# Routing loop: low halves on two engines, and one spread product per search step

## The chip, the cores and the metric

The kernel runs on one core of a Trainium2 chip. The metric is the device time of one execution in microseconds (us); the kernel before takes 1208.9 us in the median of three runs (1208.22 to 1209.22). The core has TensorE (PE in the profile; its weight loads are PEld), VectorE (DVE), ScalarE (ACT), GpSimd (POOL), and SyncE (SP), whose queue issues the plain DMA transfers. Each engine works through its own instructions in the order in which they were written; where one needs the result of another engine, it waits, and all behind it on that engine waits with it.

## The reference

Attention with a top-32 mask comes first (4 batches, 8 heads, 576 rows, 64 columns). Its output, 2304 tokens of 512 numbers, goes to eight experts: all token-expert scores are sorted from high to low, and a token goes to an expert if the token is still free and the expert has fewer than 288. Each expert computes max(x w1, 0) w2. At the end stands a rational function between two products with w_in and w_out.

```python
logits = x @ w_gate
order = np.argsort(-logits.flatten())
for idx in order:
    tok, e = int(idx) // E, int(idx) % E
    if assigned[tok] >= 0 or counts[e] >= cap:
        continue
    assigned[tok] = e
    counts[e] += 1
for e in range(E):
    h = np.maximum(x[assigned == e] @ w1[e], 0.0)
    out[assigned == e] = h @ w2[e]
# then: h = out @ w_in; g = P(h) / Q(|h|); result = g @ w_out
```

## The kernel before, in words

The products of the experts are exact to some 22 bits: each fp32 factor is scaled by a power of two and split into two fp16 halves, high and low, and three fp16 products are summed. For expert 0 the split of w1 and w2 (128 partitions x 4096 columns each) is made while the routing runs. `add_first` (line 1413) plans it: ScalarE writes the high half in chunks of 1024 columns (`conv_hi`, line 1357); for each block of 256 columns TensorE forms diag x raw - high in PSUM (`product`, line 1422: an fp32 product with a diagonal matrix of the scale, and an fp16 product with minus the identity), and ScalarE copies the result as the low half (`copy`, line 1428). These are 16 blocks for w1 and 16 for w2. The products use two PSUM banks in turn. When a weight's copies are done, `stage` (line 1398) fetches four more pieces of w_out into the room of the raw weight; these are the eight staged pieces.

The routing (`route`, line 1621) assigns tokens without sorting, in seven phases. In each phase `search` (line 1546) finds the score at which an expert becomes full, in four steps. A step compares all 2304 scores with 32 thresholds on VectorE (`cmp`, in two halves of nine columns), counts the hits per expert with 18 small matmuls, which follow one that subtracts what is needed (lines 1493 to 1509), lets VectorE mark which thresholds are over (`over`, line 1572, a tile of 32 partitions with nine columns), and spreads the weighted sum of these marks to all partitions with a matmul (`spread`, line 1551); VectorE makes the next 32 thresholds from it (`thr`, line 1584). In step i the spread sums the marks of steps 0 to i, with weights 1/32, 1/1024 and so on, so that it is a chain of i + 1 matmuls. The early ones of the chain are issued ahead of the marks of the last step. Between two phases VectorE runs a dozen short instructions (lines 1589 to 1678), GpSimd forms the selection, and 18 matmuls (line 1666) count it.

All other work near the routing is planned by a small list scheduler in Python, `Flow` (line 30). A task has an engine (A is ScalarE, V is VectorE, P is TensorE), an estimated cost, tasks it needs, and a rank; of the tasks that could start, the one with the earliest start and then the lowest rank is issued. In the search, `fill` (line 107) issues V tasks that fit into a budget (0.6 between cmp and over, 0.37 between over and thr, in the planner's units) and any A task that can start by then; `tail` (line 119) issues one P task after each spread. The plan of a step does not depend on whether a P task is in it. The preparation of w_in and w_out is planned the same way (`add_block`, line 420): pieces of 512 columns go through ScalarE (lines 374 to 386: the heads of a piece, with three ring buffers for some of them), VectorE (lines 396, 409, 413, for most pieces in two halves of 256 columns), ScalarE again (the norm, line 307), and in the end a split into high (line 437) and low halves (line 441, VectorE, longer than the budgets of the search). After the routing, the tokens of expert 0 are gathered, expert 0's products run, and the remaining blocks are finished beside them (`early`, line 148); then the pairs of hidden columns of the last two products follow for all experts (from line 2263).

Of the kernel before, what the change touches and what calls it, by code (L numbers as in the profile page):

```python
# [8 lines left out]
F32 = mybir.dt.float32  # L9
BF16 = mybir.dt.bfloat16  # L10
# [5 lines left out]
OP = mybir.AluOpType  # L16
# [13 lines left out]
class Flow:  # L30
# [69 lines left out]
    def use(self, cost):  # L100
        self.free["V"] += cost
        return self.free["V"]
# [69 lines left out]
def take(task, users, n, leave):  # L172

    task.takes.append((users, n))
    if not hasattr(task, "leaves"):
        task.leaves = {}
    task.leaves[id(users)] = leave
# [7 lines left out]
def kernel(  # L185
# [15 lines left out]
    nc = tc.nc  # L201
    B, H, S, D = q.shape
    N, DM = out.shape
    E = w_gate.shape[1]
    F1 = w1.shape[2]
    F2 = w_in.shape[1]
    P = 128
# [27 lines left out]
    consts = ctx.enter_context(tc.tile_pool(name="consts", bufs=1))  # L235
# [24 lines left out]
    GR = 32  # L260
    iota_r = consts.tile([P, GR], F32, name="iota_r")
    nc.gpsimd.iota(iota_r, pattern=[[1, GR]], base=0, channel_multiplier=0, allow_small_or_imprecise_dtypes=True)
    ITS, ITS_SLOW = 4, 7
    grids = consts.tile([P, ITS, GR], F32, name="grids")
    weights = consts.tile([GR, ITS], BF16, name="weights")
    fine_slow = consts.tile([P, ITS_SLOW], F32, name="fine_slow")
    for i in range(ITS):
        nc.vector.tensor_scalar(grids[:, i, :], iota_r, 1.0, float(GR) ** -(i + 1), op0=OP.add, op1=OP.mult)
        nc.vector.memset(weights[:, i : i + 1], float(GR) ** -(i + 1))
    for i in range(ITS_SLOW):  # L270
        nc.vector.memset(fine_slow[:, i : i + 1], 1.0 / (GR - 2) ** (i + 1))

# [38 lines left out]
    w_raw = {}  # L311
# [10 lines left out]
    w_sum, w_scale, w_split = {}, {}, {}  # L322
# [9 lines left out]
    flow = Flow()  # L332
# [3 lines left out]
    def fetch(slot, n=None):  # L336

        if n is None and todo and todo[0] <= slot[1]:
            n = todo.pop(0)
        if n is not None:  # L340
            nc.sync.dma_start(slot[0].bitcast(U16)[:, 0:2047], pieces[n][:, 1:2048])
            raw_t[n] = slot
            arrived[n].end = flow.transfer(1.5)
        elif slot[2] is not None:
            slot[2]()
# [130 lines left out]
    with ExitStack() as actx:  # L476
# [852 lines left out]
        def add_steps(steps, deps, rank, late=False):  # L1329

            done = []
            for engine, cost, fn, *takes in steps:
                t = flow.add(engine, cost, fn, deps, rank, late)
                if done and done[-1][1]:
                    take(done[-1][0], pa_users, 2, [t])
                done.append((t, takes))
                deps = [t]
            return deps[0]

        def scale_steps(which, e):  # L1340
            st = {}

            def total():
                st["t"] = ps_a.tile([P, 512], F32, name="pa")
                nc.tensor.matmul(st["t"][:, 0:4], ones, w_sum.pop((which, e)), start=True, stop=True)

            def reduce():
                w_scale[which, e] = [lpool.tile([P, 1], F32, name=f"w{n}{which}", bufs=5) for n in "si"]
                n2 = lpool.tile([P, 1], F32, name="wnorm", bufs=2)
                nc.vector.tensor_reduce(n2, st["t"][:, 0:4], axis=AX.X, op=OP.add)  # L1350
                st["steps"] = power_steps(*w_scale[which, e], n2, 380 + 2 * (11, 13)[which - 1])

            return [("P", 0.3, total, 1), ("V", 0.1, reduce)] + [
                ("V", 0.07, lambda i=i: st["steps"][i]()) for i in range(4)
            ]

        def conv_hi(which, e, c):
            if c == 0:
                w_split[which, e] = [lpool.tile([P, KC * F1], F16, name=f"w{which}s{i}") for i in range(2)]
            o = slice(c * 1024, (c + 1) * 1024)  # L1360
            nc.scalar.activation(w_split[which, e][0][:, o], w_raw[which, e][:, o], AF.Copy, scale=w_scale[which, e][0])
# [36 lines left out]
        def stage(which):  # L1398
# [11 lines left out]
            for i in range(4):  # L1410
                fetch((t[:, 1024 * i : 1024 * (i + 1)], -1, after), NP - 8 + 4 * (which - 1) + i)

        def add_first(which):

            scaled = add_steps(scale_steps(which, 0), [], -90.0)
            diag = npool.tile([P, P], F32, name=f"diag{which}", bufs=1)
            copies = [flow.add("A", 0.1, lambda: nc.scalar.activation(
                diag, ident, AF.Copy, scale=w_scale[which, 0][0]
            ), [scaled], -88.0)]
            bank = {}  # L1420

            def product(o):
                (h, l), src = (t[:, o : o + 256] for t in w_split[which, 0]), w_raw[which, 0][:, o : o + 256]
                pl = bank[o] = ps_l.tile([P, 512], F32, name="pl")[:, 0:256]
                nc.tensor.matmul(pl, diag, src, start=True, stop=False)  # L1425
                nc.tensor.matmul(pl, minus, h, start=False, stop=True)

            def copy(o):
                nc.scalar.activation(w_split[which, 0][1][:, o : o + 256], bank.pop(o), AF.Copy)

            for c in range(4):
                t = flow.add("A", 0.95, lambda c=c: conv_hi(which, 0, c), [scaled], -88.0)
                for o in range(c * 1024, (c + 1) * 1024, 256):
                    p = flow.add("P", 0.6, lambda o=o: product(o), [t, copies[0]], -88.0)
                    copies.append(flow.add("A", 0.27, lambda o=o: copy(o), [p], -90.0))
                    take(p, pl_users, 2, [copies[-1]])
            return flow.add("A", 0.0, lambda: stage(which), copies, -90.0)
# [20 lines left out]
        def routing(x, xs, lg, span, fast):  # L1458

            with ExitStack() as rctx:  # L1460
                rp = rctx.enter_context(tc.tile_pool(name="rp", bufs=1, side="right"))
                rw = rctx.enter_context(tc.tile_pool(name="rw", bufs=2, side="right"))
                psr = rctx.enter_context(tc.tile_pool(name="psr", bufs=2, space=PSUM))
# [43 lines left out]
                def compare(pc, need):  # L1507

                    nc.tensor.matmul(pc, ones_row[:, 0:GR], need[0:1, :], start=False, stop=True)

                CS = "9 9".split()
                CT, o = [], NT
# [33 lines left out]
                def search(edge, grid, vt, oh, need, fill, tail, use, until):  # L1546

                    rng, base = grid[0:2]
                    thr, overs = base[:, 0, :], []

                    def spread(pb, i, last):
                        nc.tensor.matmul(
                            pb, weights[:, i : i + 1].to_broadcast([GR, P]), overs[i], start=(i == 0), stop=last
                        )

                    for it in range(ITS):
                        if it == ITS - 1:
                            flow.free["G"] = max(flow.free["G"], flow.free["V"] + 4.5)
                        pc = counted(thr, vt, oh, need if it else None)
                        if it == 0:  # L1560
                            need, rest = need()
                            compare(pc, need)
                            rest()
                            use(0.4)
                        counts = use(C1) + 0.6
                        pb = psr.tile([P, 512], F32, name="pt")[:, 0 : E + 1]
                        for i in range(it):
                            spread(pb, i, False)
                        fill(J1 if it else J3)
                        until(counts)  # L1570
                        over = rw.tile([GR, E + 1], BF16, name="over8", bufs=ITS)
                        nc.vector.tensor_scalar(
                            over[:, 1:], pc, 0.0, None, op0=OP.is_ge, op1=OP.max, accum_out=over[:, 0:1]
                        )
                        overs.append(over)
                        spread(pb, it, True)
                        sums = use(0.07) + 0.36
                        tail(T1)
                        fill(J2)
                        until(sums)  # L1580
                        use(0.3)
                        if it < ITS - 1:
                            thr = rw.tile([P, GR], F32, name="thr")
                            nc.vector.scalar_tensor_tensor(
                                thr, rng.to_broadcast([P, GR]), pb[:, 0:1], base[:, it + 1, :], op0=OP.mult, op1=OP.add
                            )
                        else:
                            full = rw.tile([P, E], F32, name="full")
                            nc.vector.tensor_scalar(full, pb[:, 1:], pb[:, 0:1], None, op0=OP.is_equal)
                            nc.vector.tensor_scalar(edge, rng, pb[:, 0:1], span[:, 0:1], op0=OP.mult, op1=OP.add)  # L1590
                    return full
# [885 lines left out]
    with tc.If(nc.values_load(unusual[0:1, 0:1], min_val=0, max_val=P) != 0, preferred_fallthrough_block=False):  # L2477
# [7 lines left out]
        flow = Flow()  # L2485
# [40 lines left out]
```

## Time and profile before

| | before |
|---|---|
| median of three runs | 1208.9 us |
| the profiled execution, its own time | 1211.95 us |
| its span, first to last instruction | 1210.1 us |
| mean granted TensorE clock | 0.928 |

A window query sums, for each engine, the time in which it was busy in a stretch of the span; in a timeline row stand the start, the duration, the engine, the line, the operation, output<-input, and in brackets the idle time before with what ended it. "x2" stands for two like instructions in a row, whose duration then reaches from the first's start to the last's end. The granted clock is given in parts of full speed: 0.50 is the lower level, 1.2 GHz, and 1.00 the upper, 2.4 GHz.

### The profile page before, as it was taken

How to read it: one execution, taken by the hardware profiler on the slowest of the kernel's cores; microseconds unless marked ns; L12 is line 12 of the kernel's file. 1: busy time of each engine (PE TensorE's matmuls, PEld its weight loads, DVE VectorE, ACT ScalarE, POOL GpSimd, SP SyncE). 2: the span in 40 equal slices, each digit the busy share in tenths (PEclk: the TensorE clock that was granted, in tenths of full speed). 3: DMA queues.
4: the chain of work that ended last, by engine and by line, in shares of the span. 5: the costliest groups of instructions: out<-in, count | busy, mean ns of one | idle time of the engine just before them, and what ended most of it. 6: DMA issues, size and time to landing. Idle time of an engine off the chain costs nothing.

```text
span 1210.1 us, 26891 instructions
## 1 busy us (share of the span) xinstructions
PE 1118.0 (92%) x9758; PEld 902.8 (75%) x9758; DVE 1045.9 (86%) x4036; ACT 1019.4 (84%) x1816; POOL 385.6 (32%) x488
## 2 busy tenths in 40 slices
PE   5899999999999887995669999999999999999995
PEld 3688888888888765664547778888888888888774
DVE  6999999989889956878899888998989899897885
ACT  4899999989999796579999888888889887876684
POOL 4788888877778600003000010110000110001010
PEclk8899999999999995555889999999999999999998
DMA  5205212022000307413141302222211222000000
GB/s 126 53 10 157 46 25 51 23 48 51 3 2 2 140 1 281 159 54 100 62 159 71 140 27 86 88 90 78 97 66 32 90 91 84 8 2 21 1 21 23
DMA packets 81248, 80.64 MB, mean 67 GB/s; under 512 B 59985, under 2 KB 60113, under 8 KB 81105
## 3 DMA queue, kind: packets, MB, share of 16 engines
q1 hardware_dynamic: 78032, 69.34, 18.0%
q0 software_dynamic: 3072, 9.48, 2.7%
q8 instruction: 79, 1.29, 0.4%
q14 instruction: 65, 0.52, 0.1%
HBM read 69.25 MB, written 9.55 MB: 65 GB/s over the span
## 4 chain that ended last, share of the span: by engine, by line
PE 60%; DVE 18%; ACT 13%; issue 3%; POOL 3%; DMA 1%; SPq 0%; POOLq 0%; ACTq 0%; DVEq 0%
PE po L887 5%; PE po L2024 4%; PE po L2025 4%; PE po L2023 4%; PE ph L2023 4%; PE pa L2023 4%; PE ph L2025 4%; PE ph L2024 4%; PE pa L2024 4%; PE pa L2025 4%; DVE cd L753 4%; PE s L696 3%; PE pt L855 3%; DVE w L790 2%; PE pl L1425 2%
## 5 line engine op out<-in xcount | busy, mean ns | idle before, releaser
L789 POOL TENSOR_TENSOR win<-sv,sg 128x576 f32<-128x576 f32 x142 | 179.1, 1282 | 64.9 <-ACT sg L784 49.3
L753 DVE MAX8 cd<-sv 128x8 f32<-128x82 f32 (+1 forms) x1008 | 178.2, 230 | 11.5 <-ACT sv L706 11.4
L2023 PE MATMUL ph<-x,win 128*128 128x288 f16 x512 | 148.6, 290 | 7.2 <-DVE uv L2292 6.1
L887 PE MATMUL po<-vm,pT 128*128 128x65 f32 (+1 forms) x1280 | 150.7, 266 | 2.3 <-issue 1.1
L2024 PE MATMUL ph<-x,win 128*128 128x288 f16 x512 | 148.6, 290 | 0.0
L2025 PE MATMUL ph<-x,win 128*128 128x288 f16 x512 | 148.5, 290 | 0.0
L2024 PE MATMUL po<-g,wout 128*128 128x288 f16 x512 | 146.4, 286 | 2.3 <-DVE g L2014 2.3
L2023 PE MATMUL po<-g,wout 128*128 128x288 f16 x512 | 146.4, 286 | 1.4 <-ACT g L2013 1.3
L2025 PE MATMUL po<-g,wout 128*128 128x288 f16 x512 | 146.4, 286 | 0.0
L887 PEld LDWEIGHTS po<-vm,pT 128*128 128x128 f32 (+1 forms) x1280 | 138.6, 181 | 5.5 <-issue 1.9
L855 PE MATMUL pt<-ident,sv 128*128 128x128 f32 x648 | 125.7, 283 | 0.3 <-ACT pT L869 0.3
L859 PE MATMUL pt<-dg,mk 128*128 128x128 bf16 x720 | 120.0, 221 | 0.7 <-POOL mk L846 0.7
L2000 POOL DMA_INDIRECT xe<-xrows,rows_i x24 | 28.5, 1189 | 285.2 <-PE pa L2035 265.0
L784 ACT ACTIVATE sg<-sv,cut_all 128x576 bf16<-128x576 f32 x142 | 109.0, 778 | 5.7 <-DVE cut_all L759 5.7
L2283 ACT ACTIVATE z<-ph,inv 128x288 f32<-128x288 f32 x128 | 63.7, 497 | 57.8 <-PE ph L2025 54.9
L2413 POOL DMA_INDIRECT out_dram<-ob,tok x21 | 23.2, 1104 | 277.3 <-ACT ob L2409 223.0
L845 ACT ACTIVATE sg<-sv,pn 128x576 bf16<-128x576 f32 x136 | 97.9, 771 | 14.9 <-POOL pn L823 14.9
L696 PE MATMUL s<-region 64*128 64x288 f32 (+1 forms) x640 | 95.0, 450 | 14.9 <-ACT region L667 10.3
L790 DVE MAX8 w<-win 128x8 f32<-128x576 f32 x142 | 105.4, 743 | 0.0
L855 PEld LDWEIGHTS pt<-ident,sv 128*128 128x128 f32 x648 | 92.5, 143 | 15.8 <-issue 3.5
L846 POOL TENSOR_SCALAR mk<-sg 128x576 bf16<-128x576 bf16 x136 | 88.9, 671 | 1.8
L869 ACT ACTIVATE pT<-pt 128x1152 f32<-128x1152 f32 x72 | 81.4, 1131 | 3.1 <-PE pt L859 2.9
(364 smaller groups left out, 3309.2 us busy)
## 6 DMA issues: line engine op xcount, KB each, us to landing
region<-in_moe_w_dram SPq DMA_DIRECT2D x16, 2048.0 KB, 8.3
xrows<-x SPq DMA_DIRECT2D x1, 4644.0 KB, 21.8
region<-in_q_dram SPq DMA_DIRECT2D x32, 128.0 KB, 3.0
region<-in_k_dram SPq DMA_DIRECT2D x32, 128.0 KB, 3.0
vm<-in_v_dram SPq DMA_DIRECT2D x32, 128.0 KB, 3.1
wout<-in_moe_w_in_dram SPq DMA_DIRECT2D x8, 511.8 KB, 7.9
region<-in_moe_w_out_dram SPq DMA_DIRECT2D x8, 511.8 KB, 3.5
win<-in_moe_w_in_dram SPq DMA_DIRECT2D x6, 511.8 KB, 7.5
```

Source lines behind the costliest of these rows:

```text
L696: nc.tensor.matmul(sc[p0 : p0 + n, 2 * hh + g, 0:w], qT[rows, j, p0 : p0 + n], kT[rows, bb, c : c + w], start=True, stop=True,)
L753: nc.vector.max(cd[:, g, :], sv[:, o : o + n])
L784: nc.scalar.activation(sg, sv_t[u, hh], AF.Sign, bias=cut_all[:, 2 * u + hh, 7:8], scale=-OVER, accum_out=t["sum"][:, c : c + 1],)
L789: nc.gpsimd.tensor_tensor(win, sv_t[u, hh], sg, op=OP.mult)
L790: later.append(lambda c=c, win=win: nc.vector.max(t["w8"][:, c, :], win))
L845: nc.scalar.activation(sg, sv, AF.Sign, bias=t["pn"][:, c : c + 1])
L855: nc.tensor.transpose(dst, pr[:, c * P : (c + 1) * P], ident)
L859: nc.tensor.matmul(dst, mk_buf[u % 2][:, o : o + P], bat[b]["dg"][:, 2 * i + hh, :], start=False, stop=True, skip_group_check=True,)
L887: nc.tensor.matmul(po[p0 : p0 + n, i, hh, :], sb[:, hh * (R + 1) + c, p0 : p0 + n], vm[:, bb, hh, c, :], start=(c == 0), stop=False,)
L2023: nc.tensor.matmul(acc, ah, bh, start=first, stop=False)
L2024: nc.tensor.matmul(acc, ah, bl, start=False, stop=False)
L2025: nc.tensor.matmul(acc, al, bh, start=False, stop=last)
```

## The change

In `add_first`, of the blocks of 256 columns every second one (odd block numbers) no longer goes through TensorE and ScalarE: VectorE makes the low half from raw weight, scale and high half in one instruction. In `search`, the marks of the four steps stand in one tile of 128 partitions, 32 per step, and the weights in one column of 128 partitions, so that one matmul over 32, 64, 96 or 128 partitions takes the place of the chain of spreads.

```diff
-    weights = consts.tile([GR, ITS], BF16, name="weights")
+    weights = consts.tile([P, 1], BF16, name="weights")
...
-        nc.vector.memset(weights[:, i : i + 1], float(GR) ** -(i + 1))
+        nc.vector.memset(weights[GR * i : GR * (i + 1), :], float(GR) ** -(i + 1))
...
+        def rest_of(which, o):
+            h, l = w_split[which, 0]
+            nc.vector.scalar_tensor_tensor(
+                l[:, o], w_raw[which, 0][:, o], w_scale[which, 0][0], h[:, o], op0=OP.mult, op1=OP.subtract
+            )
+
...
                 for o in range(c * 1024, (c + 1) * 1024, 256):
+                    if o // 256 % 2:
+                        copies.append(flow.add("V", 0.37, lambda o=o: rest_of(which, slice(o, o + 256)), [t], -88.0))
+                        continue
                     p = flow.add("P", 0.6, lambda o=o: product(o), [t, copies[0]], -88.0)
...
-                    thr, overs = base[:, 0, :], []
-
-                    def spread(pb, i, last):
-                        nc.tensor.matmul(
-                            pb, weights[:, i : i + 1].to_broadcast([GR, P]), overs[i], start=(i == 0), stop=last
-                        )
-
+                    thr = base[:, 0, :]
+                    overs = rw.tile([GR * ITS, E + 1], BF16, name="over8")
...
-                        pb = psr.tile([P, 512], F32, name="pt")[:, 0 : E + 1]
-                        for i in range(it):
-                            spread(pb, i, False)
...
-                        over = rw.tile([GR, E + 1], BF16, name="over8", bufs=ITS)
+                        over = overs[GR * it : GR * (it + 1), :]
...
-                        overs.append(over)
-                        spread(pb, it, True)
+                        pb = psr.tile([P, 512], F32, name="pt")[:, 0 : E + 1]
+                        nc.tensor.matmul(
+                            pb, weights[0 : GR * (it + 1), :].to_broadcast([GR * (it + 1), P]),
+                            overs[0 : GR * (it + 1), :], start=True, stop=True,
+                        )
```

## Rows read from the trace of the kernel before

**Rows 1.** The page's first part: busy time, share of the span, instructions.
```profile
PE 1118.0 (92%) x9758; PEld 902.8 (75%) x9758; DVE 1045.9 (86%) x4036; ACT 1019.4 (84%) x1816; POOL 385.6 (32%) x488
```
**Rows 2.** Windows: routing, and what follows; stretch, length, busy by engine, clock, DMA.
```profile
core 0: us, PE busy (x) PEld busy (x) DVE busy (x) ACT busy (x) POOL busy (x), PEclk, DMA share, GB/s
...
462.30:555.20 92.90, 80.72 (x911) 55.53 (x912) 70.75 (x321) 67.63 (x113) 6.43 (x15) 0.50 0.46 165
555.20:645.00 89.80, 61.00 (x402) 43.82 (x402) 83.16 (x213) 85.63 (x158) 13.50 (x9) 0.82 0.31 103
```
**Rows 3.** Timeline, VectorE: a search step of the first phase.
```profile
466.38 0.26 DVE L1584 SCALAR_TENSOR_TENSOR thr<-rng,pt,base 128x32 f32<-128x32 f32 x1 [0.19 <-PE pt L1552]
466.67 0.83 DVE L1493 TENSOR_TENSOR cmp<-vt,thr 128x288 bf16<-128x288 f32 x2
...
467.99 0.16 DVE L1572 TENSOR_SCALAR_CACHE_REDUCE over<-pl 32x8 bf16<-32x8 f32 x1
...
468.41 0.26 DVE L1584 SCALAR_TENSOR_TENSOR thr<-rng,pt,base 128x32 f32<-128x32 f32 x1 [0.20 <-PE pt L1552]
```
**Rows 4.** Timeline, TensorE and VectorE: a search step of the second phase.
```profile
476.98 1.22 PE L1425 MATMUL pl<-region,diag 128*128 128x256 f32 x2
477.10 0.25 DVE L1584 SCALAR_TENSOR_TENSOR thr<-rng,pt,base 128x32 f32<-128x32 f32 x1
...
478.00 0.42 PE L1426 MATMUL pl<-w1s,minus 128*128 128x256 f16 x1
...
478.55 0.64 PE L1501 MATMUL pl<-oh,cmp 128*32 128x8 bf16 x18
479.12 0.49 PE L1552 MATMUL pt<-over,weights 32*128 32x9 bf16 x3
479.23 0.16 DVE L1572 TENSOR_SCALAR_CACHE_REDUCE over<-pl 32x8 bf16<-32x8 f32 x1 [0.68 <-PE pl L1501]
...
479.66 0.25 DVE L1584 SCALAR_TENSOR_TENSOR thr<-rng,pt,base 128x32 f32<-128x32 f32 x1
```
**Rows 5.** Waits (total, times, longest) and ScalarE's group of w2 copies, routing.
```profile
DVE over L1572 <- PE pl L1501: 11.4, 18, 0.7
ACT w1s L1429 <- PE pl L1426: 10.7, 8, 2.2
DVE nq L428 <- ACT junk L307: 2.0, 2, 1.7
...
L1429 ACT ACTIVATE w2s<-pl 128x256 f16<-128x256 f32 x16 | 6.2, 388 | 7.4 <-PE pl L1426 7.4
```
**Rows 6.** Groups of VectorE, 470 to 546 us: busy us, mean ns.
```profile
L396 DVE SCALAR_TENSOR_TENSOR ring<-wout,ring 128x256 uint16<-128x256 uint16 x16 | 7.0, 437 | 0.0
L409 DVE SCALAR_TENSOR_TENSOR wout<-wout,ring 128x256 uint32<-128x256 uint32 x16 | 6.6, 413 | 0.0
...
L409 DVE SCALAR_TENSOR_TENSOR win<-win 128x256 uint32<-128x256 uint32 x6 | 2.5, 414 | 0.0
```
**Rows 7.** Timeline: the end of the last phase.
```profile
545.21 0.67 PE L1666 MATMUL pt<-asel,onesb 128*128 128x8 bf16 x18
...
545.92 0.16 DVE L1678 TENSOR_TENSOR need<-cb,pt 128x8 f32<-128x8 f32 x1 [0.86 <-PE pt L1666]
```
**Rows 8.** VectorE after the loop: a timeline row, and two groups by line.
```profile
559.17 0.75 DVE L409 SCALAR_TENSOR_TENSOR nraw<-nraw,ring 128x256 uint32<-128x256 uint32 x2
...
L441 DVE SCALAR_TENSOR_TENSOR win<-wout,s_in,win 128x512 f16<-128x512 f32 x8 | 5.7, 733 | 0.0
...
L1366 DVE SCALAR_TENSOR_TENSOR w1s<-region,ws,w1s 128x1024 f16<-128x1024 f32 x8 | 10.1, 1276 | 0.0
```
**Rows 9.** ScalarE's group of staged pieces, and VectorE's waits, after the loop.
```profile
L384 ACT ACTIVATE region<-region 128x512 int8<-128x512 bf16 x4 | 5.4, 1341 | 0.0
...
DVE wout L441 <- ACT wout L437: 1.9, 1, 1.9
...
DVE hT L2010 <- ACT hT L2009: 1.0, 2, 0.5
```
**Rows 10.** Timeline, ScalarE: the first activation of the pair loop.
```profile
613.90 0.50 ACT L2283 ACTIVATE z<-ph,inv 128x288 f32<-128x288 f32 x1 [2.21 <-DVE inv L2161]
```

## The prediction, made before the changed kernel ran

> **What bounds the kernel now.** I read the engine totals first. The TensorE matmul row is busy 92% of the span, VectorE 86%, ScalarE 84% [rows 1]: no engine is spare on average, so the answer lies in single stages. The table of windows comes next [rows 2]. The routing loop runs from 462.3 to 555.2 us, at a granted clock of 0.50, the lower level (1.2 GHz). TensorE is busy 80.7 of its 92.9 us, VectorE 70.8, ScalarE 67.6. From 555.2 to 645 it turns: ScalarE is busy 85.6 and VectorE 83.2 of 89.8 us, TensorE only 61.0. So the change sits in a serial loop, and what the loop leaves undone is worked off behind it by two engines that are nearly full.
>
> The timeline inside the loop shows what a search step costs. One step is the distance between two thr instructions on VectorE. In the first phase, where TensorE carries no product of a w1 or w2 block, it is 468.41 - 466.38 = 2.03 us [rows 3]. In a step with a product it is 479.66 - 477.10 = 2.56 us [rows 4]. The reason is TensorE's order: the product's two fp32 passes (1.22 us) and its fp16 pass (0.42 us) run from 476.98 to 478.42, and the 18 counting matmuls, whose compares were ready earlier, begin only at 478.55. The wait table says the same in total: VectorE's over waits for the counting 18 times, 11.4 us, while ScalarE's copies wait for the products (10.7 us for w1 alone) [rows 5]. A product in a step is therefore worth 2.56 - 2.03 = 0.53 us of the serial chain. That ScalarE is in the chain only through TensorE is plain from its waiting there.
>
> **The products that go.** There are 32 products, two matmul instructions deep each, and 16 leave. Before, two run at the first phase boundary and five in each of phases 2 to 7: three in search steps (18 such waits in [rows 5]), two at the phase boundary. The planner still issues one per gap in the same order, so 16 are used up by 2 + 5 + 5 + 4, that is in phase 4. Phases 5, 6 and 7 lose 9 products that sit in steps: 9 x 0.53 = 4.8 us. At a phase boundary VectorE's own chain of a dozen small instructions goes on beside the two products, and I take nothing there, with one exception: at the end of the last phase the 18 matmuls of L1666 start at 545.21 behind a product, and VectorE waits 0.86 us for them [rows 7]. About 0.6 of that is the product and goes. Routing: -4.8 - 0.6 = -5.4 us.
>
> **The 16 instructions that VectorE gains.** The trace has none of 256 columns with these operands. From below, the shift-and-or of 256 columns (L409) takes 413 ns [rows 6]. From above, the same arithmetic on 512 columns takes 733 ns and on 1024 columns 1276 ns [rows 8]; the slope between them carried to 256 columns gives 0.46 us, which is an estimate, and I use 0.41 to 0.46 because both are close. In the loop such an instruction is free where it falls, since each step has two gaps on VectorE (before over and before thr) that already hold instructions of 413 to 437 ns in steps of 2.56 us, and a step without a product still leaves 0.49 us from the end of cmp (466.67 + 0.83) to over at 467.99 [rows 3]. But these gaps are full: 16 + 16 + 6 half-block instructions for w_in and w_out, in the three largest groups alone, stand in them from 470 to 546 us [rows 6], two per step, with small ones in the rest. The new instructions are ranked ahead of these, so 16 halves are pushed behind the loop. There they cost what halves back to back cost, 0.75 us for two with the overlap, some 0.335 us each [rows 8]: 16 x 0.335 = +5.4 us on VectorE. The bounds are 0 (all fall into idle time) and 16 x 0.46 = 7.4.
>
> The idle time behind the loop is small but there: VectorE waits for ScalarE 1.9 and 1.0 us at two lines [rows 9], and ScalarE waits at the start of the pair loop 2.2 us for VectorE [rows 10], so VectorE ends this part. Work that is ready can fall into such gaps. I let it take 2.0 of the 2.9 us, so that 3.4 of the 5.4 us are paid.
>
> **ScalarE** loses 16 copies, 0.39 us each by the mean of the w2 ones [rows 5], 6.2 us; but it waited in the loop anyway. What moves with the displaced halves (their norms, the heads of the next pieces, limited by three ring buffers) goes behind the loop, while the pieces staged into the freed weights arrive earlier, and their conversions (1.34 us for the first of three, where the plan reckons 0.52 [rows 9]) move from behind the loop into it. I count these against each other: 0, with -3 to +4 as the bounds.
>
> **One spread for four.** Six of the ten spread matmuls of a phase go. Before, the early ones follow the counting matmuls and run while VectorE makes over: those of the third step take 0.49 us from 479.12 with the last one [rows 4], and the thr that reads them starts at 479.66, 0.43 us after over (479.23), as against 0.42 in the step of [rows 3]. The last of them waits for over before and after. So 0 is taken; at the most 0.05 us a step, 1.4 us in all, could be gained, and the same lost if over, now written 32, 64 or 96 partitions lower than it is read, is slower, which no row shows. The other edits (weights on 128 partitions, four memsets) run once: 0.
>
> The row says that three spreads of 32 rows take three times the issue of one. The Trainium skill ("TensorE: Matmul & The Clock Gate", Why this matters for your kernels) says that a product over 32 rows takes the same time as one over 128. By it the merged product costs one spread, and the sum would be the same, since the early spreads lie beside over; by the opposite, a product of 128 rows costing four, each fourth step would grow by up to 0.3 us, some 2 us in all.
>
> **The sum.** -5.4 (loop) + 5.4 (halves later) - 2.0 (idle filled) = -2.0 us. The profiled execution took 1211.95 us (span 1210.1 and 1.85 around it), 3.05 above the median of the runs, 1208.9. It gives 1209.95 for the profiled one and 1206.9 us on the median's scale.
>
> **The rivals.**
> - *The halves are free.* ScalarE ends the stage behind the loop (85.6 against 83.2 us busy [rows 2]), so VectorE's 5.4 us hide under it, and the loop's gain stays whole: 1208.9 - 5.4 = 1203.5. For it speaks the ScalarE row; against it, that ScalarE waits for VectorE just where the pair loop begins.
> - *Nothing is left.* The halves cost their 5.4 us, no idle time takes them up: 1208.9.
> - *ScalarE holds up the loop: slower.* VectorE is in order, and a fill that needs ScalarE stalls the search: the norm sum L428 already waits 2.0 us in two places, 1.7 of it in phase 6, where four staged pieces were being converted [rows 5]. With the products gone early, all eight staged pieces are converted within the loop, in steps 0.53 us shorter, with the plan's price too low [rows 9]. If that stall comes four times rather than once, it costs 3 x 1.7 = 5.1 us: the loop gains only 0.3 and the halves still cost 3.4 to 5.4 behind it, some +3.1 to +5.1, about 1213. It decides from the point where ScalarE has more to do in a phase than the phase lasts, which the present 67.6 of 92.9 us [rows 2] do not reach on the whole but may in phases 4 to 7.
> - *The change frees no step*, because the planner puts other products into the gaps or spreads the 16 over all phases: then no step gets shorter and the halves cost 3.4: 1212.3. Nothing in the loop's queue speaks for it.
>
> **How the numbers follow.** Forecast 0.40, free halves 0.23, nothing left 0.14, ScalarE in the loop 0.19, no step freed 0.04. The likeliest gives 1206.9, with a range of its own of 1204.5 to 1209. A measurement of this kernel can tell about 0.2%, 2.4 us, from no change; the forecast's 2.0 lies within it. Faster by more: half of the forecast's case less a little (0.18), the free halves (0.23) and a bit of the rest, 0.42. Slower by more: 0.19 + 0.04 and a little, 0.24. Same: 0.34. The range reaches from the free halves, with some of the ScalarE bound, 1202.8, to the slower cases, 1212.8.
>
> **What would show it.** Phases 5 to 7 of the changed kernel should have steps of 2.03 to 2.1 us, and phases 2 to 4 still 2.56; 16 half-block instructions should be missing from the loop and stand behind it; the loop should end some 5.4 us earlier, and the first size activation of the pair loop (613.9 before) some 2 us earlier. A norm sum that waits for ScalarE several times in the loop would show the slower rival; a VectorE with more idle time behind the loop than before would refute the price of the halves. The prediction is wrong if the steps without a product are no shorter, or if the pair loop moves by much more or less than the sum.

## The result, and the profile after

The changed kernel takes 1219.89 us in the median of six runs (1218.12 to 1222.45), beside 1209.62 us for the kernel before on the same chip: ratio 1.0078, 95% interval 1.0061 to 1.0094, 7.4 to 11.4 us slower. The forecast was 1206.9 us, with a range of 1202.8 to 1212.8: sign and range were both missed. The profiled execution took 1221.22 us, 9.27 more than the one before.

The page's first row, which answers to [rows 1], shows a TensorE that has 23.5 us less to do, and nothing gained by it:

```profile
PE 1094.5 (90%) x9668; PEld 891.2 (73%) x9668; DVE 1054.2 (86%) x4052; ACT 1013.8 (83%) x1800; POOL 383.1 (31%) x488
```

The stages tell more. Here are three windows each: from the first over of the routing to its last, from there to the asg instruction that ends the assignment, and from that to the first activation of the pair loop. The columns are the stretch and its length, the busy time of TensorE, its weight loads, VectorE, ScalarE and GpSimd, the granted clock, and the DMA share and GB/s. First the kernel before, then the changed one:

```profile
463.87:542.60 78.73, 72.82 (x812) 49.05 (x812) 61.45 (x284) 55.91 (x99) 5.02 (x11) 0.50 0.50 183
542.60:546.87 4.27, 3.19 (x28) 2.18 (x28) 2.78 (x16) 3.55 (x7) 1.40 (x3) 0.50 0.13 32
546.87:613.90 67.03, 41.38 (x304) 30.88 (x303) 59.66 (x153) 62.77 (x110) 13.50 (x9) 0.74 0.25 80
```

```profile
465.80:545.59 79.79, 54.19 (x730) 39.86 (x730) 64.45 (x286) 56.53 (x84) 5.03 (x11) 0.50 0.50 186
545.59:549.24 3.65, 0.79 (x19) 0.67 (x19) 2.86 (x16) 0.04 (x1) 1.41 (x3) 0.50 0.00 0
549.24:623.23 73.99, 39.69 (x294) 29.26 (x294) 65.97 (x177) 60.41 (x115) 11.10 (x9) 0.69 0.21 68
```

The loop is 1.06 us longer, its tail 0.62 shorter, the stretch behind it 6.96 longer: +7.40 us. The remaining 1.87 of the 9.27 us are 1.93 ahead of the loop (465.80 against 463.87), -0.23 behind the first activation, and 0.17 outside the span. Ahead of the loop both kernels run the same instructions (but for where the four memsets of the weights write), and over the kernels below the loop began anywhere from 461.92 to 466.38 in the one profile that each has. So I compare stages, and not whole spans, between profiles.

In the loop, the nine steps of phases 5 to 7 took 24.15 us before, a stall of 1.1 among them, and take 19.42, with a stall of 0.5: most of the forecast gain is there. But one step of phase 4 takes 8.38 instead of 2.56 us. VectorE's timeline in it:

```profile
502.58 0.16 DVE L1573 TENSOR_SCALAR_CACHE_REDUCE over<-pl 32x8 bf16<-32x8 f32 x1 [0.96 <-PE pl L1510]
...
503.40 0.83 DVE L1502 TENSOR_TENSOR cmp<-vt,thr 128x288 bf16<-128x288 f32 x2
510.38 0.16 DVE L428 TENSOR_REDUCE nq<-nq 128x1 f32<-128x4 f32 x1 [6.15 <-ACT junk L307]
...
510.96 0.17 DVE L1573 TENSOR_SCALAR_CACHE_REDUCE over<-pl 32x8 bf16<-32x8 f32 x1
```

and ScalarE's at the same time:

```profile
503.66 2.46 ACT L384 ACTIVATE region<-region 128x512 int8<-128x512 bf16 x2
505.86 2.52 ACT L385 ACTIVATE region<-region 128x512 bf16<-128x512 bf16 x2
508.13 1.32 ACT L386 ACTIVATE region<-region,bias 128x512 uint32<-128x512 uint16 x2
509.35 0.36 ACT L1435 ACTIVATE w2s<-pl 128x256 f16<-128x256 f32 x1
509.62 0.64 ACT L307 ACTIVATE junk<-win 128x512 bf16<-128x512 f32 x1
```

VectorE has compared and the counting matmuls are done by 505.4, but ahead of over in VectorE's queue stands a fill (a task that the planner put into the gap): the sum of four norms of a w_in block (L428). It needs the norm that ScalarE makes at 509.62, and ahead of that in ScalarE's queue stand the conversions of two staged pieces of w_out, 6 us of work. This is the wait of [rows 5] again, 1.7 us at its longest there and 6.15 here. The pieces are staged into the raw weights' room, which is free sooner when half of the products are gone: the transfer of the last of the eight pieces is issued at 514.92 instead of 545.24 us.

What is pushed out of the loop can be counted. Here are VectorE's groups in the loop of the changed kernel, to be set beside [rows 6] (the columns are busy us, mean ns, idle before):

```profile
L396 DVE SCALAR_TENSOR_TENSOR ring<-wout,ring 128x256 uint16<-128x256 uint16 x10 | 4.4, 440 | 0.1
L1415 DVE SCALAR_TENSOR_TENSOR w1s<-region,ws,w1s 128x256 f16<-128x256 f32 x8 | 3.8, 478 | 0.1
L1415 DVE SCALAR_TENSOR_TENSOR w2s<-region,ws,w2s 128x256 f16<-128x256 f32 x8 | 3.8, 478 | 0.1
L409 DVE SCALAR_TENSOR_TENSOR wout<-wout,ring 128x256 uint32<-128x256 uint32 x9 | 3.8, 422 | 0.2
```

In the loop L396 falls from 16 to 10 (and one more, on nraw, from 1 to 0), and L409 on wout from 16 to 9: 14 halves stand behind the loop instead. These groups behind the loop, and that of a low half, first before, then after:

```profile
L396 DVE SCALAR_TENSOR_TENSOR ring<-nraw,ring 128x256 uint16<-128x256 uint16 x7 | 2.9, 433 | 0.0
...
L441 DVE SCALAR_TENSOR_TENSOR wout<-region,s_out,wout 128x512 f16<-128x512 f32 x4 | 2.7, 739 | 0.0
...
L396 DVE SCALAR_TENSOR_TENSOR ring<-wout,ring 128x256 uint16<-128x256 uint16 x4 | 1.6, 431 | 0.0
L409 DVE SCALAR_TENSOR_TENSOR wout<-wout,ring 128x256 uint32<-128x256 uint32 x4 | 1.5, 412 | 0.0
```

```profile
L409 DVE SCALAR_TENSOR_TENSOR wout<-wout,ring 128x256 uint32<-128x256 uint32 x11 | 4.2, 413 | 0.0
L396 DVE SCALAR_TENSOR_TENSOR ring<-wout,ring 128x256 uint16<-128x256 uint16 x10 | 4.0, 437 | 0.0
L441 DVE SCALAR_TENSOR_TENSOR wout<-region,s_out,wout 128x512 f16<-128x512 f32 x5 | 3.5, 740 | 0.0
L396 DVE SCALAR_TENSOR_TENSOR ring<-nraw,ring 128x256 uint16<-128x256 uint16 x8 | 3.3, 439 | 0.0
```

VectorE is busy 6.3 us more behind the loop: 5.5 for the 14 halves by their groups, and 0.8 for one more low half of 512 columns (L441). The stretch grows by 7.0, so VectorE's idle time in it grows too, from 7.37 to 8.02 us. ScalarE, which before had four staged pieces to convert as the loop ended, has none left and waits for a half that comes only behind the loop:

```profile
558.89 0.67 ACT L307 ACTIVATE junk<-wout 128x512 bf16<-128x512 f32 x1 [13.26 <-DVE wout L409]
```

### The profile page after: what moved, and what is told of

Same layout as the page of the kernel before. It is cut to its first block, busy times and chain, and to the rows that moved or that the text cites. A ratio compares the mean times of both kernels' runs of the same rounds, so it can differ in the third digit from the quotient of the medians.

```text
span 1219.2 us, 26717 instructions
## 1 busy us (share of the span) xinstructions
PE 1094.5 (90%) x9668; PEld 891.2 (73%) x9668; DVE 1054.2 (86%) x4052; ACT 1013.8 (83%) x1800; POOL 383.1 (31%) x488
## 4 chain that ended last, share of the span: by engine, by line
PE 58%; DVE 19%; ACT 15%; POOL 3%; issue 3%; DMA 2%; SPq 0%; POOLq 0%; ACTq 0%; DVEq 0%
PE po L887 5%; PE ph L2027 4%; PE po L2028 4%; PE ph L2029 4%; PE ph L2028 4%; PE po L2029 4%; PE po L2027 4%; PE pa L2027 4%; PE pa L2028 4%; PE pa L2029 4%; DVE cd L753 4%; PE s L696 3%; PE pt L855 3%; DVE w L790 2%; ACT junk L307 2%
```

## Experiments

The theory after the result is that the blocks alone cost the time, in two places: a stall of 6 us, because conversions that the plan prices too low come before norms, and 16 new instructions on VectorE that push others out of the loop, which is paid behind it. The rivals are that the merged spread costs the time; that ScalarE has too much to do, whatever the plan; and that ScalarE's late idle time, and not VectorE's work, lengthens the stretch behind. In all that follows, "before" without a label is the kernel before, with the stages 78.73, 4.27 and 67.03 us.

**The merged spread alone** (label e1): the changed kernel without the new branch.

```diff
-                    if o // 256 % 2:
-                        copies.append(flow.add("V", 0.37, ...rest_of...))
-                        continue
```

> The merged spread alone, all 32 products on TensorE as before. Theory (the loss comes from the blocks alone; the early spreads lay beside over): within 1.5 us of before, search steps 2.56 us with a product as before. Rival (the merged spread or the shifted write of over is what costs): 3 us or more slower, and steps longer than 2.56 us.

Ratio 0.9992 (0.9976 to 1.0008), loop 78.69 us, behind it 67.09. With all 32 products in place the merged spread does nothing to the time: the theory holds here, its rival falls. (The steps with a product are 2.56, 2.56 and 2.47 us in most phases.)

**The blocks alone** (e2): the kernel before with rest_of and the new branch.

> The odd blocks on VectorE alone, spreads in chains of up to four as before. Theory: some 10 us slower than before, like the whole change, with one stall of some 6 us in the loop where VectorE's norm sum waits for ScalarE. Rival (merged spread): at most 5 us slower.

Ratio 1.0057 (1.0038 to 1.0075), a step of 8.28 us with a wait of 6.26 for the norm, loop 79.88, behind it 73.46. The stages are those of the whole change (79.79 and 73.99). By the ratio it is 6.9 us slower (4.6 to 9.1): less than the 10 that were expected, and the interval just reaches the 5 us that the rival allowed, so it is the stages and e1 that decide against the rival.

**The plan with truer prices** (e3): the whole change, one line of add_block different.

```diff
-  t = [flow.add("A", (0.52, 0.52, 0.61)[k], lambda n=n, k=k: heads(n)[k][2](), t, rank + 0.5, late)]
+  t = [flow.add("A", (1.36, 1.36, 0.7)[k], lambda n=n, k=k: heads(n)[k][2](), t, rank + 0.5, late)]
```

> The whole change, and the planner reckons the three head conversions of a piece at 1.36, 1.36 and 0.70 instead of 0.52, 0.52 and 0.61, near what ScalarE takes. Theory (the stall comes from these conversions being planned too cheaply in front of the norms): the long stall goes, the loop from the first to the last over becomes some 5 us shorter than before, the stretch behind it stays 6 to 7 us longer: 1 to 4 us slower than before. Rival (ScalarE has too much to do in the loop, whatever the plan): the stall only moves, still 8 us or more slower.

Ratio 1.0030 (1.0014 to 1.0046), 1.7 to 5.6 us slower. VectorE's wait for the norm is 1.23 us, and the windows are

```profile
462.37:536.44 74.07, 54.06 (x730) 39.92 (x730) 64.41 (x286) 55.10 (x84) 5.02 (x11) 0.50 0.54 202
536.44:540.10 3.66, 0.80 (x19) 0.67 (x19) 2.87 (x17) 0.04 (x1) 1.41 (x3) 0.50 0.00 0
540.10:615.32 75.22, 39.37 (x293) 28.93 (x293) 66.38 (x177) 60.57 (x115) 10.05 (x9) 0.68 0.22 67
```

The loop is 4.66 us shorter than before, and with the tail 5.27. ScalarE does nearly the same work in it as in the changed kernel (55.10 against 56.53 us), in another order: it did not have too much to do. What is left is the stretch behind, 8.2 us longer than before, where 6 to 7 were expected. How much of both differences comes from the new prices alone, e6 shows.

**Without the odd blocks** (e5): the same plan, the low halves of the odd blocks left at zero.

```diff
                     if o // 256 % 2:
-                        copies.append(flow.add("V", 0.37, ...rest_of...))
                         continue
...
+            odd = w_split[which, 0][1].rearrange("p (n a c) -> p n a c", a=2, c=256)[:, :, 1, :]
+            nc.gpsimd.memset(odd, 0.0)
```

> The whole change with the head conversions reckoned at 1.36, 1.36 and 0.70 (as in the run before it), and the low halves of the odd blocks of expert 0's w1 and w2 left out: GpSimd fills them with zeros ahead of the routing, VectorE's 16 instructions are gone. Theory (the stretch behind the loop is longer because these 16 push halves of w_in and w_out behind it): the loop stays some 5 us shorter than before, the stretch behind it comes back from 75.2 to within 1.5 us of 67.0: 4 to 6 us faster than before. Rival (that stretch is longer because ScalarE stands idle late in the loop and its work comes after): it stays above 71 us, and the kernel is at most 2 us faster than before.

Ratio 0.9956 (0.9941 to 0.9971), 3.5 to 7.1 us faster than before.

```profile
462.48:536.10 73.62, 54.23 (x730) 39.77 (x730) 62.85 (x287) 61.40 (x96) 6.78 (x12) 0.50 0.55 202
536.10:539.75 3.65, 0.79 (x19) 0.66 (x19) 2.87 (x17) 0.04 (x1) 1.41 (x3) 0.50 0.00 0
539.75:606.85 67.10, 40.10 (x302) 30.46 (x301) 60.17 (x150) 53.58 (x102) 9.24 (x9) 0.74 0.23 74
```

With the 16 instructions gone, the stretch behind the loop is 67.10 us, as before, and 8.1 less than with them: 0.51 us for each. VectorE's busy time there falls by 6.2 (66.38 to 60.17), ScalarE's by 7.0. So the longer stretch needs the 16 instructions, and the rival falls. The granted clock of the stretch differs too, 0.68 with them and 0.74 without; but in e7 below it is 0.70, and the stretch takes 67.13 us. The 1.9 us beyond VectorE's work are idle time of VectorE, 8.84 us with the instructions and 6.93 without; among its waits, the one for ScalarE's conversions at L409 grows from 0.3 to 1.5 us. Whether that comes from ScalarE's share in the displaced pieces or from their order was not separated. Nor were the instructions left out at the changed kernel's own prices.

**The truer prices on the kernel before** (e6): the line of e3, nothing else.

> The kernel before with nothing but the head conversions reckoned at 1.36, 1.36 and 0.70. Theory (before, the cheap plan cost one stall of 1.7 us in phase 6, and the order behind the loop hardly depends on it): between 2 us faster and 1 us slower. Rival (the new costs by themselves spoil the order behind the loop, so that the longer stretch of the run with the whole change and these costs is theirs): the stretch behind the loop is 3 us or more longer than 67.0, and the kernel 2 us or more slower.

Ratio 1.0007 (0.9996 to 1.0017).

```profile
463.37:540.78 77.41, 72.55 (x812) 49.15 (x812) 61.37 (x284) 55.39 (x99) 5.02 (x11) 0.50 0.51 186
540.78:545.06 4.28, 3.19 (x28) 2.18 (x28) 2.78 (x17) 3.57 (x7) 1.41 (x3) 0.50 0.16 29
545.06:614.33 69.27, 40.19 (x304) 30.57 (x303) 60.17 (x153) 62.07 (x110) 9.81 (x9) 0.75 0.24 78
```

The stall of phase 6 is gone (loop 77.41), and the stretch behind is 2.2 us longer (69.27): nothing in all. Both numbers lie on the theory's side of their bounds, but the second shows that new prices move the order behind the loop too.

This run is also the fair partner of e3, since both have the same prices. Between them the change shortens the loop by 3.34 us and the tail by 0.62, and lengthens the stretch behind by 5.95, with VectorE busy 6.21 us more in it: 2.0 us slower by the stages. So 1.3 of the 4.66 us that e3's loop gains, and 2.2 of the 8.2 that its stretch behind loses, belong to the prices.

**The odd blocks on GpSimd** (e7): before, with e3's prices, and

```diff
+        def rest_of(which, o):
+            h, l = w_split[which, 0]
+            r = w_raw[which, 0][:, o]
+            nc.gpsimd.tensor_scalar(r, r, w_scale[which, 0][0], None, op0=OP.mult)
+            nc.gpsimd.tensor_tensor(l[:, o], r, h[:, o], op=OP.subtract)
...
+                    if o // 256 % 2:
+                        copies.append(flow.add("G", 1.0, lambda o=o: rest_of(which, slice(o, o + 256)), [t], -88.0))
+                        continue
```

> The odd blocks on GpSimd instead of VectorE (scale the raw block in place, subtract the high half: two instructions a block), chains of spreads as before, head conversions reckoned at 1.36, 1.36 and 0.70. Theory (VectorE's full gaps are what made the change slow; GpSimd is idle in the loop): the loop 4 to 5 us shorter than before, the stretch behind it within 1.5 us of before: 3 to 5 us faster than before. Rival (GpSimd's instructions hold up VectorE's beside them, as they do with vt, 0.40 instead of 0.17 us): steps of phases 2 and 3 longer than 2.6 us, and not faster than before.

Ratio 1.0013 (1.0002 to 1.0024). The stretch behind is 67.13 us, as the theory has it, but the loop takes 80.86: the boundary of phases 2 and 3 took 10.49 us. GpSimd's timeline there:

```profile
490.25 0.93 POOL L1416 TENSOR_SCALAR region<-region,ws 128x256 f32<-128x256 f32 x1
491.26 0.67 POOL L1417 TENSOR_TENSOR w2s<-region,w2s 128x256 f16<-128x256 f32 x1
491.89 0.43 POOL L1672 TENSOR_TENSOR asel<-oh,gone 128x144 bf16<-128x144 bf16 x1
```

The selection that the search needs (asel) follows a queue of blocks without a gap. A block was planned at 1.0 and takes 1.16 + 0.77 us by the means of its two groups. It is the fault of the change once more, a price too low ahead of an instruction on the chain. The theory's forecast failed, and what the rival named came true as well: three steps of phases 2 and 3 took 2.65 to 2.90 us (last section), and the kernel is not faster. Which of the two weighs more, the next run shows.

**The same at a price of 2.0** (e8):

```diff
-                        copies.append(flow.add("G", 1.0, lambda o=o: rest_of(which, slice(o, o + 256)), [t], -88.0))
+                        copies.append(flow.add("G", 2.0, lambda o=o: rest_of(which, slice(o, o + 256)), [t], -88.0))
```

> As the run with the odd blocks on GpSimd, but the planner reckons a block at 2.0 instead of 1.0 there (its two instructions took 1.16 and 0.77 us), so that it plans no more blocks ahead of a phase boundary than GpSimd can finish. Theory (the 10.5 us boundary of that run was GpSimd's queue in front of the selection, and nothing else was lost): boundaries back to 4.1 to 4.6 us, loop 74 to 76 us, the stretch behind it within 1.5 us of before: 3 to 5 us faster than before. Rival (GpSimd slows VectorE beside it by more than the freed steps give): loop above 77 us, within 1.5 us of before.

Median 1205.65 us beside 1211.67 for the kernel before, ratio 0.9946 (0.9931 to 0.9962).

```profile
466.38:541.22 74.84, 58.09 (x772) 41.16 (x772) 69.33 (x287) 61.61 (x96) 36.19 (x43) 0.50 0.54 199
541.22:544.75 3.53, 0.92 (x22) 0.73 (x22) 2.78 (x16) 0.17 (x1) 1.41 (x3) 0.50 0.02 5
544.75:611.85 67.10, 39.52 (x302) 30.13 (x301) 60.17 (x150) 53.62 (x102) 9.25 (x9) 0.74 0.22 74
```

By the ratio it is 6.5 us faster than before (4.6 to 8.4), more than the 3 to 5 that were expected, and this version beats both kernels: 3.9 us in the loop, 0.7 in its tail, and nothing given back. The boundary of phases 2 and 3 is back from 10.49 to 4.40 us, so it was GpSimd's queue (the one of phases 1 and 2 stays at 4.94, where 4.1 to 4.6 were expected). Of the 3.9 us, 1.3 belong to the prices (e6). GpSimd's 36.2 busy microseconds replace TensorE's products without taking a gap from VectorE.

**Every fourth block on VectorE** (e9): e3 with

```diff
-                    if o // 256 % 2:
+                    if o // 256 % 4 == 3:
```

> The whole change with the corrected head costs, but only every fourth block on VectorE: 8 instead of 16. Theory (each such block pushes about one half-block instruction behind the loop, 0.5 us by the run without them; each freed search step gives 0.53): loop 75 to 77 us, the stretch behind it 70 to 72 us: 0 to 2 us slower than before, about half of the way between 32 products and 16. Rival (the first few go into gaps that are empty, only the later ones push): the stretch behind the loop within 1.5 us of before, 2 us or more faster than before.

Loop 75.22, tail 3.54, stretch behind 70.49 us: with 8 instructions the stretch is 3.5 us longer than before, 0.43 each, near half of what 16 cost. Against the run with the same prices and the same 8 blocks on GpSimd (e10, 67.11) it is 3.4 longer, so the price is paid from the first ones on, and no empty gaps take them; against e6, where TensorE and ScalarE still make these blocks, it is only 1.2. The stages sum to 0.8 us less than before; the ratio is lower, 0.9975 (0.9965 to 0.9986), 3.0 us faster, where 0 to 2 slower was expected.

**Every fourth block on GpSimd** (e10): the same edit in e8.

> As the run with GpSimd blocks reckoned at 2.0, but only every fourth block on GpSimd, 8 in all. Theory: the loop frees four search steps and the stall of phase 6, 75 to 77 us, the stretch behind it as before: 1.5 to 3.5 us faster than before. Rival (half as much of GpSimd's work beside VectorE is better than all of it): as fast as or faster than the run with 16 blocks.

Ratio 0.9946 (0.9927 to 0.9965), loop 76.38, behind 67.11. By the stages 8 blocks gain 3.0 us and 16 gain 4.6, by the ratios both gain 6.5, more than the 1.5 to 3.5 expected for 8; whether 16 are better is not settled. In this last set, e8 to e10, the ratios show 2 to 3.5 us more gain than the stages. Their before ran at 1211.67 in the median against 1209.62 in the first set; what lies in the difference outside the three stages is not known.

## Why the prediction was wrong

- **Where the bound lies**: right. A product in a step costs 0.53 us, and the nine steps that were freed are those of phases 5 to 7 that were named; without one a step takes 2.03 or 2.15 us. From 24.15 to 19.42 us is -4.73, the forecast -4.8, but that they agree so closely is luck: 0.6 of the 4.73 is a shorter stall. Where no stall stands among the nine steps, in e6 and e3, they go from 23.0 to 19.0 us, -4.05; the missing 0.7 is the merged spread's (below).
- **The tail**: -0.62, forecast -0.6.
- **ScalarE, "against each other: 0, with -3 to +4"**: this step failed first. The working added up ScalarE's work and left out the order of its queue. The pieces staged earlier did move into the loop, as it said, but in front of a norm on which a fill waits, and the fill stands before over in VectorE's queue. In phase 4 three steps take 13.71 us instead of 7.68, +6.03. One of the rivals named this wait and the too low price, at four stalls of 1.7 us and a chance of 0.19; it came as one of 6.15. That rival let it hang on ScalarE having more to do than a phase lasts; but with truer prices in the plan the wait shrank to 1.23 at nearly the same work (e3), so it is the order, not the amount.
- **The halves, "+5.4, of which idle time takes 2.0"**: the direction was right, and the second term failed. 3.4 us were to be paid behind the loop; the stretch grew by 6.96 in the changed kernel, and by 8.1 against the same plan without the instructions (e5). The 5.4 itself came near by two errors that cancel: 14 halves and not 16 went behind the loop, at 0.39 us each and not 0.335, 5.5 in all. To them came 0.8 for one low half. The idle time took up nothing: VectorE's idle time there grew by 0.65 us (7.37 to 8.02), which the prediction had named as the sign against its price of the halves. So of the 3.56 us that were missed, 2.0 are idle time that was counted on, 0.65 idle time that came new, and 0.9 more work of VectorE.
- **The merged spread**: 0 forecast, and 0.9992 (0.9976 to 1.0008) measured where every product is in place (e1). In the freed steps it costs something: the nine steps take 19.0 us in e3, which has the merged spread, and 18.3 in e8, which has the chains, 0.7 us that the forecast has at nothing (it had named up to 1.4 as a bound). The last section shows where they arise. The product itself is not slower: over 32, 64, 96 or 128 partitions it takes 0.16 to 0.17 us. The reading that three spreads take three times the issue of one was wrong: of the chain of three in [rows 4], the trace has the starts at 479.12, 479.17 and 479.45 us, so the first two follow each other by 0.05 us, and the last one waits for over.
- **The 16 new instructions**: 0.41 to 0.46 us each were estimated; they take 478 ns, a little above the bounds.

With 6.03 for the stall instead of 0 and 6.96 instead of 3.4 for the stretch behind, the sum of -2.0 becomes +7.6; the stages show +7.4. The other 2 us of the measured 9.4 lie outside the three stages, and their cause is open.

## What to carry to other kernels

When work moves to an engine whose gaps in a serial loop are full, it is not free where it lands: count what stands in the gaps now, and price that where it will go, with the chain of engines it brings along. When a plan is written out by estimated prices, each price that is too low is a queue in front of something, so look up, for everything that becomes available earlier, which in-order instruction will stand behind it. Here this cost 6 us in the change, and 6 again on GpSimd; a truer number in the plan took away nearly all of the first and all of the second. An engine that is idle in the loop (here GpSimd, 5 of 79 us busy) could take the same work without pushing anything out, though VectorE's instructions beside it ran slower. And when two plans are compared, compare them at the same prices: the new prices alone moved one stage by 1.3 us and another by 2.2.

## What the runs showed of the hardware

Behind an over that is written to partitions 32 and up, VectorE's next instruction starts later. In the changed kernel, in a step without a product:

```profile
519.72 0.16 DVE L1573 TENSOR_SCALAR_CACHE_REDUCE over<-pl 32x8 bf16<-32x8 f32 x1
519.81 0.07 DVE L1573 DVE_READ_ACCUMULATOR over<-pl 32x1 bf16 x1
519.92 0.43 DVE L413 TENSOR_TENSOR win<-win 128x256 f32<-128x256 f32 x1
...
520.26 0.25 DVE L1588 SCALAR_TENSOR_TENSOR thr<-rng,pt,base 128x32 f32<-128x32 f32 x1
```

In the kernel with the blocks alone (e2), where over is written to the partitions from which it is read:

```profile
518.25 0.16 DVE L1581 TENSOR_SCALAR_CACHE_REDUCE over<-pl 32x8 bf16<-32x8 f32 x1
518.35 0.07 DVE L1581 DVE_READ_ACCUMULATOR over<-pl 32x1 bf16 x1
518.35 0.43 DVE L396 SCALAR_TENSOR_TENSOR ring<-wout,ring 128x256 uint16<-128x256 uint16 x1
...
518.69 0.24 DVE L1593 SCALAR_TENSOR_TENSOR thr<-rng,pt,base 128x32 f32<-128x32 f32 x1
```

In e2 the fill behind over starts 0.10 us after it, beside the accumulator read; in the changed kernel 0.20 us after it, when that read is over. The fill then holds up thr by as much: 0.54 against 0.44 us after over. It is not the spread: its matmul starts 0.22 us after over and takes 0.16 to 0.17 us in both kernels. In the first step of a phase, where the changed kernel too writes over to partitions 0 to 31, the next instruction starts after 0.09 us, and thr (from phase 4 on) after 0.42 to 0.43. Where the fill is a short one (0.15 us), thr starts after 0.43 to 0.44 us in the later steps too. That the write to other partitions than those read is the cause fits all these rows, but it was not tried by itself.

Many of VectorE's instructions are slower beside GpSimd. In the run with the blocks on GpSimd (e7) the w_in halves in phases 2 and 3 took 607 and 595 ns on average, where they took 415 (L413) and 414 (L409) before [rows 6]; over, which reads PSUM, stayed at 0.16 us:

```profile
L413 DVE TENSOR_TENSOR win<-win 128x256 f32<-128x256 f32 x6 | 3.6, 607 | 0.0
L409 DVE SCALAR_TENSOR_TENSOR win<-win 128x256 uint32<-128x256 uint32 x6 | 3.6, 595 | 0.0
```

Most steps hid it, since they wait for a product anyway; three in phases 2 and 3 took 2.65 to 2.90 instead of 2.56 us, and in e8 five in phases 2 to 4 took 2.64 to 2.90.
